# Two more buffers for raw words of w1 and w2 in the weights' pool, and the first two of their blocks converted in the fold's last four steps

## The chip, the cores and the metric

The kernel runs on one core of a Trainium2 chip. The metric is the device time of one execution in microseconds (us), the median of several runs; lower is better.

## The reference

Local attention over q, k, v (4 batches, 8 heads, 576 positions, head width 64; each position sees itself and the 63 before it), then two feed-forward layers on 2304 tokens:

```python
attn = softmax(mask(scale * q @ k.T)); x = heads side by side(attn @ v)   # 2304 x 512
x = ((x @ w1) * (x @ w2)) @ w3 @ w_out        # w1, w2: 512x1024, w3: 1024x1024, w_out: 1024x512
h = x @ w_in; out = maximum(0.01 * h, h) @ w_out2     # w_in: 512x2048, w_out2: 2048x512
```

q, k and v are float32. All weights arrive as 8-byte words (float64), so that each block of a weight is loaded twice as large as its float32 and has to be turned into float32 on the chip.

## The kernel before

Every product is made of three matmuls (`mm3`, L77, L78, L79: high x high, high x low, low x high), since each operand is split into a rounded high part and the low rest. The kernel has three stages; this case lies in the first two.

**The fold** (first 95 us). w3 @ w_out is multiplied out ahead of the tokens. It takes 16 steps (`its`); in each, `w3_tr` turns one block of w3 (TensorE L470, high part by ScalarE L472, low part by VectorE L473, both into a tile `w3T`), and `w3_mm` multiplies (tiles `mm`). The results are copied out as `wf` at L493 and L494.

**The token chunks.** Five chunks of tokens (`c` = 0 to 4), and in each eight column blocks `f`. `ab_step` multiplies x by a block of w1 (part 0, copied out by ScalarE at L669 as `a`) and of w2 (part 1, multiplied with `a` at L674, split at L675 and L676); `y_step` multiplies the result by `wf`. PSUM has two tiles `ab` for the products of `ab_step`, `w3_tr` and some transposes, taken in turn. The attention of later chunks is put between these steps by a plan (`plan_att`, `slot`): scores `sc` L245, their maximum `nm` on VectorE L249, exponent on ScalarE L253, scaling on GpSimd L263, transposes L276 copied out at L279, and the product with v L306, copied out at L309 and L310. `prep_k` (L229) and `prep_q` (L236) turn the keys and queries on VectorE after they were loaded (L224).

**Converting weights.** A block of a weight is a *unit*, numbered in order: 0 to 13 are w3 and w_out, 14 and 15 are the first 256 columns of w1 and w2, 16 and 17 the second, 18 and 19 the third, 20 and 21 the last; w_in follows. From unit 4 to 21 a unit is 1 MB of words. `advance` moves units through five steps: the load (SP's queue, L382), *scale* (ScalarE, L417 and L391, in place on the words), *shift* (VectorE, L438), *sign* (VectorE, L396), and *fin*: for w1 and w2 ScalarE writes the high part (L332) and GpSimd the low part (L333) of a tile `w`. A unit is loaded when `n_of["bits"]`, the number of units that have passed *sign*, has reached its `after` value, since it overwrites the words of an earlier one. w1 and w2 take turns in two places, `raw_at(0, 2)` and `raw_at(2, 2)`.

All loads are issued by SP, in order, on one queue. The semaphores of that queue are eight (DMAHW0 to DMAHW7), taken in turn: a load waits until the load eight places ahead of it has landed. A scheduler sets the order of the instructions on each engine when the kernel is built; each engine then runs its own list strictly in that order. The tiles' pool `wpool` has eight slots with the tag `w`: four for `wo` (w_out) and four for the first two blocks of w1 and w2; later blocks take the slots of `wo`.

Of the kernel before, what the change touches and what calls it, by code (L numbers as in the profile page):

```python
# [11 lines left out]
I64 = mybir.dt.int64  # L12
# [9 lines left out]
def tile_kernel(ctx: ExitStack, tc: tile.TileContext, q, k, v, w1, w2, w3, w_out, w_in, w_out2, out):  # L22
# [18 lines left out]
    P = 128  # L41
# [17 lines left out]
    UC = 512  # L59
# [9 lines left out]
    def f32(ap):  # L69
        return ap.bitcast(F32)  # L70
# [11 lines left out]
    wpool = tc.alloc_tile_pool(name="wpool", bufs=1)  # L82
# [229 lines left out]
    def wslot(key):  # L312
        pl, tag, bufs = wpool, "w", 8
        if key[0] == "wo2":
            pl, tag, bufs = (po1, "w1", 4) if key[1] < 4 else (po2, "w2", 4)
        elif key[0] == "wf":
            tag, bufs = "wf", 4
        return pl.tile([P, 2, 2 * UC], F32R, name=tag, tag=tag, bufs=bufs)

    def rows2(t):  # L320
        return t.rearrange("p s (l m) -> p s l m", l=2)
# [17 lines left out]
    slots = {}  # L339
# [11 lines left out]
    def part_of(kind, dims, dt=F32):  # L351

        n = 1
        for d in dims:
            n *= d
        if words_in is not None:
            return words_in.tile([P] + list(dims), dt, name=kind, tag=kind, bufs=RAW)
        i = n_of[kind] % RAW
        n_of[kind] += 1
        x = {"raw": raw_all, "f": f_all}[kind][:, i].bitcast(dt)[:, 0:n]  # L360
        return shaped(x, dims)

    def feed():

        while n_of["load"] < n_of["cap"] and n_of["bits"] >= units[n_of["load"]]["after"]:
            load_unit()
# [22 lines left out]
    def low_bits(raw, n=UC):  # L389

        act.activation(out=raw.bitcast(I32).rearrange("p (m two) -> p m two", two=2)[:, :, 0],  # L391
                       in_=raw.bitcast(U8).rearrange("p (m e) -> p m e", e=8)[:, :, 3],
                       func=AF.Copy, scale=1.0 / 32, bias=-31.0 / 64)

    def sign(f, hi):
        dve.scalar_tensor_tensor(out=f, in0=hi, scalar=-0x80000000, in1=f, op0=ALU.bitwise_and, op1=ALU.bitwise_or)  # L396

    def f_free(i):

        if i >= PHASE_B:  # L400
            return True
        a, n = units[i]["f_at"]
        for j in range(i):
            b, m = units[j]["f_at"]
            if a < b + m and b < a + n and (n_of["fin"] <= j or not units[j]["free"]()):
                return False
        return True

    def advance(stop):

        now = dict(n_of)
        if now["scale"] < min(stop, now["load"]):
            u = units[now["scale"]]
            w = u["raw"].bitcast(I32).rearrange("p (m two) -> p m two", two=2)
            u["lo"], u["hi"] = w[:, :, 0], w[:, :, 1]
            if now["scale"] < PHASE_B:
                act.mul(u["hi"].bitcast(F32), u["hi"].bitcast(F32), 2.0 ** -112)  # L417
                low_bits(u["raw"])
            else:
                u["f"] = part_of("f", [UC])  # L420
                with tc.issue_after(pss["copy"]):
                    act.mul(u["f"], u["hi"].bitcast(F32), 2.0 ** -112)
            n_of["scale"] += 1
        if now["fin"] < now["bits"]:
            u = units[now["fin"]]
            u["fin"](u["f"])
            n_of["fin"] += 1
        d = now["bits"] < now["shift"]
        if d:
            u = units[now["bits"]]  # L430
            f = u["f"].bitcast(I32)
            sign(f, u["hi"])
        if now["shift"] < now["scale"] and f_free(now["shift"]):
            u2 = units[now["shift"]]
            if now["shift"] < PHASE_B:
                i, n = u2["f_at"]
                u2["f"] = f_all[:, i:i + n].rearrange("p n m -> p (n m)")
                dve.scalar_tensor_tensor(out=u2["f"].bitcast(I32), in0=u2["hi"], scalar=3, in1=u2["lo"],  # L438
                                         op0=ALU.logical_shift_left, op1=ALU.bitwise_or)
            else:  # L440
                g = u2["f"].bitcast(I32)
                dve.tensor_scalar(g, g, 3, 0x7FFFFFF8, op0=ALU.logical_shift_left, op1=ALU.bitwise_and)
            n_of["shift"] += 1
        if d:
            if now["bits"] >= PHASE_B:
                dve.scalar_tensor_tensor(out=f, in0=u["lo"], scalar=29, in1=f, op0=ALU.logical_shift_right, op1=ALU.bitwise_or)
            n_of["bits"] += 1
            feed()
# [28 lines left out]
    def w3_mm(gi, l, half):  # L477
        t = w3T[0]
        wo = rows2(slots["wo", l // 2])
        for i in range(2 * half, 2 * half + 2):  # L480
            if l == 0:
                wps[i] = ps_mm.tile([P, DM], F32, name="mm", tag="mm")
            mm3(wps[i], t[:, 0, i, :], t[:, 1, i, :], wo[:, 0, l % 2], wo[:, 1, l % 2], l == 0, l == KF - 1)
        if half == 0:
            return
        w3T.pop(0)
        if l == KF - 1:
            for i in range(2):
                if ("wf", 2 * gi + i) not in slots:
                    slots["wf", 2 * gi + i] = wslot(("wf", 2 * gi + i))  # L490
            for i in range(4):
                wf = rows2(slots["wf", 2 * gi + i // 2])
                act.copy(wf[:, 0, i % 2], wps[i])  # L493
                dve.tensor_tensor(out=wf[:, 1, i % 2], in0=wps[i], in1=f32(wf[:, 0, i % 2]), op=ALU.subtract)  # L494
# [10 lines left out]
    def raw_at(i, n):  # L505
        return lambda: raw_all[:, i:i + n].rearrange("p n m -> p (n m)")
# [3 lines left out]
    def wf_raw(i):  # L510

        def at():
            if i not in spare_raw:
                spare_raw[i] = wpool.tile([P, 2 * UC], I64, name="wf", tag="wf", bufs=4)
            return spare_raw[i]
        return at

    for l in range(2):
        unit(w3[0:4 * P, P * l:P * l + P].rearrange("(k p) m -> p k m", p=P), (lambda l: lambda f: words.update({(0, l): f.rearrange("p (k m) -> p k m", m=P)}))(l),
             ("w3", 0, l), raw_at(2 * l, 1), 0, (2 * l, 1))  # L520
        unit(w_out[P * l:P * l + P, :], store(("wo", 0), l), ("wo", l), raw_at(2 * l + 1, 1), 0, (2 * l + 1, 1))
    PLACES = [wf_raw(0), wf_raw(1), raw_at(0, 2), raw_at(2, 2)]
    AFTER = {4: 0, 5: 0, 6: 2, 7: 4}
    for gi in range(2):
        for l in range(2 if gi == 0 else 0, KF, 2):
            i = len(units)
            unit(w3[4 * P * gi:4 * P * gi + 4 * P, P * l:P * l + 2 * P].rearrange("(k p) m -> p k m", p=P), wide_w3(gi, l),
                 ("w3", gi, l), PLACES[i % 4], AFTER.get(i, i - 3), (2 * (i % 2), 2))
            if gi == 0:
                i = len(units)  # L530
                unit(w_out[P * l:P * l + 2 * P, :].rearrange("(k p) m -> p k m", p=P), store(("wo", l // 2), None),
                     ("wo", l), PLACES[i % 4], AFTER.get(i, i - 3), (2 * (i % 2), 2))
    W12 = len(units)
    for p in range(KD):
        for w, name in ((w1, "w1"), (w2, "w2")):
            i = len(units)
            unit(w[:, 2 * P * p:2 * P * p + 2 * P].rearrange("(k p) m -> p k m", p=P), store((name, p), None), (name, p),
                 PLACES[2 + i % 2], i - 3 if i < W12 + 2 else i - 1, (2 * (i % 2), 2))
    PHASE_B = len(units)

    def keep(i):
# [6 lines left out]
                 keep(2 * p + h), ("win", p, h), None, len(units) - 1 if len(units) < PHASE_B + 2 else  # L548
                 PHASE_B if len(units) < PHASE_B + 4 else len(units) - 3)
    n_of["cap"] = KEPT = len(units)  # L550
    for name, p in [("wo", i) for i in range(4)] + [(n, p) for p in range(2) for n in ("w1", "w2")] + [("wf", i) for i in range(2)]:
        slots[name, p] = wslot((name, p))

    ev = {}
    clock = {"t": 0}
# [40 lines left out]
    def slot():  # L596

        for _, n, _, f in sorted(ev.pop(clock["t"], []), key=lambda e: e[:2]):
            with ExitStack() as how:
                if f in (av, qk, tr) and clock["t"] >= PACED_FROM:  # L600
                    how.enter_context(tc.issue_after(pss["last"]))
                if f is prep_k and n > NHP or f is prep_q and n > 2 * NHP + 1:
                    how.enter_context(tc.issue_after(pss["dve"]))
                how.enter_context(tc.high_priority(offset=100))
                f(n)
        clock["t"] += 1
# [5 lines left out]
    def start_loads(i):  # L612

        if i == W12 + 1:
            dma.append(pss["load"])
# [15 lines left out]
    its = [(gi, l) for gi in range(2) for l in range(KF)]  # L631
    until(3, W12)
    w3_tr(words.pop((0, 0)))
    w3_tr(words.pop((0, 1)))
    until(4, W12)
    for c in range(NC):
        plan_att(c)
    for i, (gi, l) in enumerate(its):
        w3_mm(gi, l, 0)
        if i + 2 < len(its):  # L640
            g2, l2 = its[i + 2]
            if l2 % 2 == 0:
                until(last["w3", g2, l2], W12)
            w3_tr(words.pop((g2, l2)))
            if l2 % 2 and g2 == 0:
                until(last["wo", l2 - 1], W12)
        slot()
        w3_mm(gi, l, 1)
        slot()
    until(W12, PHASE_B)  # L650
    p0.release()
# [579 lines left out]
```

## Time and profile before

| what | value |
|---|---|
| median of 3 runs | 815.65 us (815.35 to 817.64) |
| the profiled execution | 819.47 us, its span 817.7 us |
| TensorE (PE) busy | 785.2 us, 96% |
| VectorE (DVE) | 572.2 us, 70% |
| ScalarE (ACT) | 431.7 us, 53% |
| GpSimd (POOL) | 66.6 us, 8% |
| mean granted clock of TensorE | 0.99 |

The span is the profiled execution from its first to its last instruction; 1.8 us of its time lie around it. Its time is 3.8 us above the median, so that a sum made in the profile is carried over to the median as a difference. The granted clock is 1.0 for 2.4 GHz and 0.5 for 1.2 GHz.

### The profile page before, as it was taken

To read this page: it belongs to the slowest core of one execution; us is meant where nothing else is said; L and a number is where in the kernel's file an instruction comes from. 1 tells how busy PE (TensorE), PEld (TensorE's weight loads), DVE (VectorE), ACT (ScalarE), POOL (GpSimd) and SP (SyncE) were. 2 spreads that over 40 slices of the span, in tenths; PEclk is the share of its full clock that TensorE was granted. 3 is DMA by queue.
4 is the path that set the end of the run, shared out by engine and by line. 5 is a ranking of instruction groups with operands and counts; after the bars stand their busy time and mean duration, and the time that the engine had idled before them with its cause. 6 is when DMAs were issued, how large, how long until landed. Compare 5 with 4: busy or idle time off the path is not lost.

```text
span 817.7 us, 14546 instructions
## 1 busy us (share of the span) xinstructions
PE 785.2 (96%) x5128; PEld 724.6 (89%) x5128; DVE 572.2 (70%) x1349; ACT 431.7 (53%) x964; POOL 66.6 (8%) x61
## 2 busy tenths in 40 slices
PE   5879899999999999999999999999999999999997
PEld 4657699999988888888888899999999999999997
DVE  6995778457456546885731766867767999898976
ACT  6866675344334324443611655654556866575744
POOL 1022434112101100111000000000000000000000
PEclk9899999999999999999999999999999999999999
DMA  9995557347745556888420457998998754444321
GB/s 312 216 267 123 153 165 194 67 98 167 175 105 140 131 133 164 248 256 255 137 64 0 145 176 244 315 330 307 327 322 269 231 171 143 128 132 128 114 94 53
DMA packets 190809, 147.12 MB, mean 180 GB/s; under 512 B 124304, under 2 KB 150160, under 8 KB 190736
## 3 DMA queue, kind: packets, MB, share of 16 engines
q1 hardware_dynamic: 187712, 141.34, 59.1%
q10 hardware_dynamic: 3024, 4.85, 1.6%
q8 instruction: 40, 0.66, 0.3%
q14 instruction: 33, 0.27, 0.1%
HBM read 98.96 MB, written 47.19 MB: 179 GB/s over the span
## 4 chain that ended last, share of the span: by engine, by line
PE 78%; DMA 7%; SPq 5%; ACT 3%; DVE 2%; issue 1%; POOL 0%; ACTq 0%; DVEq 0%
PE ab L77 7%; PE o L78 7%; PE o L79 7%; PE ab L79 7%; PE ab L78 7%; PE o L77 7%; PE pr L77 6%; PE pr L79 6%; PE pr L78 6%; PE mm L78 4%; PE mm L77 4%; DMA raw<-in_moe_w_dram 4%; PE mm L79 3%; PE sc L245 3%; SPq L224 2%; SPq L623 2%
## 5 line engine op out<-in xcount | busy, mean ns | idle before, releaser
L79 PE MATMUL ab<-x,w 128*128 128x512 f32 (+1 forms) x320 | 119.9, 375 | 2.9 <-POOL w L333 2.9
L77 PE MATMUL ab<-x,w 128*128 128x512 f32 (+1 forms) x320 | 119.4, 376 | 2.0 <-ACT x L309 1.1
L78 PE MATMUL ab<-x,w 128*128 128x512 f32 (+1 forms) x320 | 119.9, 375 | 0.0
L77 PE MATMUL pr<-yop,w 128*128 128x384 f32 x300 | 101.5, 338 | 2.5 <-ACT c L826 2.5
L79 PE MATMUL pr<-yop,w 128*128 128x384 f32 x300 | 101.1, 337 | 0.0
L78 PE MATMUL pr<-yop,w 128*128 128x384 f32 x300 | 101.0, 337 | 0.0
L253 ACT ACTIVATE s<-s,nm 128x128 f32<-128x128 f32 x144 | 56.3, 393 | 47.5 <-DVE nm L249 47.5
L826 ACT COPY c<-pr 128x384 f32<-128x384 f32 x95 | 45.1, 479 | 66.2 <-PE pr L79 54.1
L78 PE MATMUL o<-yop,yop 128*128 128x256 f32 x259 | 73.1, 282 | 0.0
L79 PE MATMUL o<-yop,yop 128*128 128x256 f32 x259 | 73.0, 282 | 0.0
L77 PE MATMUL o<-yop,yop 128*128 128x256 f32 x259 | 73.0, 282 | 0.0
L79 PEld LDWEIGHTS ab<-x,w 128*128 128x128 f32 x320 | 60.5, 189 | 10.9 <-POOL w L333 3.2
L77 PEld LDWEIGHTS ab<-x,w 128*128 128x128 f32 x320 | 60.5, 189 | 10.8 <-ACT x L309 1.3
L78 PEld LDWEIGHTS ab<-x,w 128*128 128x128 f32 x320 | 60.6, 189 | 8.2 <-DVE x L310 0.3
L263 POOL TENSOR_TENSOR s<-s,rs 128x512 f32<-128x512 f32 (+1 forms) x40 | 42.4, 1062 | 291.0 <-DVE rs L262 213.1
L829 DVE TENSOR_TENSOR c<-pr,c 128x384 f32<-128x384 f32 x74 | 40.9, 554 | 31.0 <-PE pr L79 19.8
L674 DVE TENSOR_TENSOR p<-ab,a 128x512 f32<-128x512 f32 (+1 forms) x40 | 25.2, 631 | 52.3 <-PE ab L79 39.1
L968 ACT CAST yop<-raw 128x256 fp32r<-128x256 f32 (+1 forms) x92 | 42.4, 485 | 35.5 <-PE o L78 34.8
L78 PE MATMUL mm<-ab,wf 128*128 128x512 f32 (+1 forms) x160 | 59.7, 373 | 0.8 <-DVE ab L676 0.8
L77 PEld LDWEIGHTS pr<-yop,w 128*128 128x128 f32 x300 | 56.4, 188 | 3.8 <-ACT c L826 3.8
L79 PE MATMUL mm<-ab,wf 128*128 128x512 f32 (+1 forms) x160 | 59.3, 371 | 0.0
L77 PE MATMUL mm<-ab,wf 128*128 128x512 f32 (+1 forms) x160 | 56.5, 375 | 0.0
(137 smaller groups left out, 1956.9 us busy)
## 6 DMA issues: line engine op xcount, KB each, us to landing
hd<-c SPq DMA_DIRECT2D x96, 192.0 KB, 4.1
raw<-hd SPq DMA_DIRECT2D x32, 512.0 KB, 3.8
raw<-in_moe_w_dram SPq DMA_DIRECT2D x11, 1024.0 KB, 5.7
raw<-in_moe_w_out_dram SPq DMA_DIRECT2D x18, 512.0 KB, 5.3
raw<-in_moe_w_in_dram SPq DMA_DIRECT2D x16, 512.0 KB, 5.2
wd<-f SPq DMA_DIRECT2D x32, 256.0 KB, 4.1
raw<-wd SPq DMA_DIRECT2D x30, 256.0 KB, 4.4
pd<-tb SPq DMA_DIRECT2D x12, 512.0 KB, 3.0
```

What stands on the lines that cost most here:

```text
L77: pe.matmul(ps, lhsT=lh, rhs=rh, start=first, stop=False, skip_group_check=more)
L78: pe.matmul(ps, lhsT=lh, rhs=rl, start=False, stop=False, skip_group_check=more)
L79: return pe.matmul(ps, lhsT=ll, rhs=rh, start=False, stop=last, skip_group_check=more).ins
L224: sp.dma_start(dst, src)
L245: pe.matmul(sc[:, t, :], lhsT=qb[:, t, :], rhs=kT[n][:, k0:k0 + P], start=True, stop=True)
L253: act.activation(out=s[:, t, :], in_=s[:, t, :], func=AF.Exp, bias=nm[:, t:t + 1], scale=-1.0, accum_out=sm[:, t:t + 1])
L263: pool.tensor_tensor(out=s[:, 0:m], in0=s[:, 0:m], in1=rs[:, 0:m].unsqueeze(2).to_broadcast([P, m, P]), op=ALU.mult)
L623: pss["load"] = sp.dma_start(dst, src).ins
L674: dve.tensor_tensor(out=p32, in0=ps, in1=pss["a"], op=ALU.mult)
L826: pss["copy"] = act.copy(self.sb[to], ps).ins
L829: pss["add"] = dve.tensor_tensor(out=self.sb[to], in0=self.ps[at], in1=self.sb[of or to], op=ALU.add).ins
L968: tied("act", lambda: act.copy(out, x))
```

## The change

Two of the eight `w` slots of the weights' pool become buffers for raw words (`raww`). Units 16 and 17 (the second blocks of w1 and w2) are loaded into them, as soon as 12 units have passed *sign*, which is also when unit 15 may be loaded. Units 18 to 21 use the two old places again. The second blocks' tiles `w` now take slots that `wo` leaves, and the last blocks' those of the raw buffers. In each of the fold's last four steps two calls of `advance` are added, which may go as far as unit 15.

```diff
--- before.py
+++ after.py
@@ -515,6 +515,9 @@
             return spare_raw[i]
         return at
 
+    def w_raw(i):
+        return lambda: slots["raw", i]
+
     for l in range(2):
@@ -531,11 +534,13 @@
     W12 = len(units)
+    PLACES_W = [raw_at(0, 2), raw_at(2, 2), w_raw(0), w_raw(1)] + 2 * [raw_at(0, 2), raw_at(2, 2)]
+    AFTER_W = [W12 + x for x in (-3, -2, -2, -2, 1, 2, 5, 6)]
     for p in range(KD):
         for w, name in ((w1, "w1"), (w2, "w2")):
             i = len(units)
             unit(w[:, 2 * P * p:2 * P * p + 2 * P].rearrange("(k p) m -> p k m", p=P), store((name, p), None), (name, p),
-                 PLACES[2 + i % 2], i - 3 if i < W12 + 2 else i - 1, (2 * (i % 2), 2))
+                 PLACES_W[i - W12], AFTER_W[i - W12], (2 * (i % 2), 2))
     PHASE_B = len(units)
@@ -548,8 +553,11 @@
     n_of["cap"] = KEPT = len(units)
-    for name, p in [("wo", i) for i in range(4)] + [(n, p) for p in range(2) for n in ("w1", "w2")] + [("wf", i) for i in range(2)]:
-        slots[name, p] = wslot((name, p))
+    for name, p in [("wo", i) for i in range(4)] + [("raw", i) for i in range(2)] + [(n, 0) for n in ("w1", "w2")] + [("wf", i) for i in range(2)]:
+        if name == "raw":
+            slots[name, p] = wpool.tile([P, 2 * UC], I64, name="raww", tag="w", bufs=8)
+        else:
+            slots[name, p] = wslot((name, p))
@@ -646,6 +654,9 @@
         slot()
         w3_mm(gi, l, 1)
+        if i + 4 >= len(its):
+            for _ in range(2):
+                advance(W12 + 2)
         slot()
     until(W12, PHASE_B)
```

The lines below the edits have numbers up to 11 higher in the changed kernel (L669 becomes L680). The scheduler's lists move as follows.

**SP, where the loads of w1 and w2 begin.** `raw_98` are the two old places, `kin_412` the keys and `qin_413` the queries of the first visit of chunk 1. Before:

```order
L382 DMA raw_98<-in_moe_w1_dram 128x4x256 [waits DMAHW6_49,DVE_49,Activation_49]
L382 DMA raw_98<-in_moe_w2_dram 128x4x256 [waits DMAHW7_49,DVE_49,Activation_49]
L224 DMA kin_412<-in_k_dram 32x8x32 [waits DMAHW0_49]
...
L224 DMA kin_412<-in_k_dram 32x6x32 [waits DMAHW7_49]
L224 DMA qin_413<-in_q_dram 32x6x32 [waits DMAHW0_49]
```

The same place in the changed kernel:

```order
L382 DMA raw_98<-in_moe_w1_dram 128x4x256 [waits DMAHW6_49,DVE_49,Activation_49]
L382 DMA raw_98<-in_moe_w2_dram 128x4x256 [waits DMAHW7_49,DVE_49,Activation_49]
L382 DMA raww_104<-in_moe_w1_dram 128x4x256 [waits DMAHW0_49]
L382 DMA raww_105<-in_moe_w2_dram 128x4x256 [waits DMAHW1_49]
L224 DMA kin_412<-in_k_dram 32x8x32 [waits DMAHW2_49]
...
L224 DMA kin_412<-in_k_dram 32x6x32 [waits DMAHW0_49]
L224 DMA kin_412<-in_k_dram 32x6x32 [waits DMAHW1_49]
L224 DMA qin_413<-in_q_dram 32x6x32 [waits DMAHW2_49]
```

Units 16 and 17 now stand right behind 14 and 15 and ahead of the keys, and the last two of the eight loads of keys wait for them. Between the last of these eight loads and the next load of a weight stood 40 loads of queries, keys and v; now there are 38.

**SP, at that next load of a weight.** The tile `raw_98` is unit 16's words before, and unit 18's in the changed kernel; `qin_1042` and `qin_1035` are the same queries. Before:

```order
L224 DMA qin_1042<-in_q_dram 32x6x32 [waits DMAHW7_49]
L382 DMA raw_98<-in_moe_w1_dram 128x4x256 [waits DMAHW0_49,DVE_49,Activation_49]
L382 DMA raw_98<-in_moe_w2_dram 128x4x256 [waits DMAHW1_49,DVE_49,Activation_49]
L382 DMA raw_98<-in_moe_w1_dram 128x4x256 [waits DMAHW0_49,DMAHW2_49,DVE_49,Activation_49]
L382 DMA raw_98<-in_moe_w2_dram 128x4x256 [waits DMAHW1_49,DMAHW3_49,DVE_49,Activation_49]
```

In the changed kernel:

```order
L224 DMA qin_1035<-in_q_dram 32x6x32 [waits DMAHW7_49]
L382 DMA raw_98<-in_moe_w1_dram 128x4x256 [waits DMAHW0_49,DVE_49,Activation_49]
L224 DMA qin_1035<-in_q_dram 32x6x32 [waits DMAHW1_49]
L224 DMA qin_1035<-in_q_dram 32x6x32 [waits DMAHW2_49]
L382 DMA raw_98<-in_moe_w2_dram 128x4x256 [waits DMAHW3_49,DVE_49,Activation_49]
```

The rows read alike; what has moved is which unit they load.

**ScalarE, around the last turned block of w3.** `w3T_837` before and `w3T_844` in the changed kernel are the high part of the fold's last block. `w_105` before and `w_107` in the changed kernel are the first block of w2 (unit 15). L417 and L391 are the *scale* of unit 16 before and of unit 18 in the changed kernel. Before:

```order
L472 CAST w3T_837<-ab_838 128x512 [waits PE_49,Activation_49]
L417 ACTIVATE raw_98<-raw_98 128x1024 [waits DMAHW0_49]
L391 ACTIVATE raw_98<-raw_98 128x1024
L279 COPY pts_829<-ab_861 128x3x4x32 [waits PE_49]
L332 CAST w_105<-f_99 128x1024 [waits DVE_49]
L493 CAST wf_935<-mm_592 128x512 [waits PE_49]
```

In the changed kernel:

```order
L417 ACTIVATE raw_98<-raw_98 128x1024 [waits DMAHW0_49]
L391 ACTIVATE raw_98<-raw_98 128x1024
L472 CAST w3T_844<-ab_845 128x512 [waits PE_49]
L279 COPY pts_836<-ab_875 128x3x4x32 [waits PE_49]
L332 CAST w_107<-f_99 128x1024 [waits DVE_49]
L332 CAST w_1075<-f_99 128x1024
```

The last cast of a block of w3 stood ahead of the *scale* that waits for a load, and now stands behind one.

## Rows read from the trace of the kernel before

**Rows 1.** The page: busy us, share of the span and instructions of each engine

```profile
PE 785.2 (96%) x5128; PEld 724.6 (89%) x5128; DVE 572.2 (70%) x1349; ACT 431.7 (53%) x964; POOL 66.6 (8%) x61
```

**Rows 2.** Chain of waits, 48 to 110 us: start us, us, what

```profile
55.48 11.75 DMA raw<-in_moe_w_dram
67.24 0.31 SPq L224
...
88.36 0.44 SPq L224
88.91 5.55 DMA raw<-in_moe_w_dram
94.48 1.14 ACT raw L417
95.61 1.02 ACT raw L391
...
97.00 0.95 ACT w L332
...
98.02 3.42 POOL w L333
101.48 0.48 PE ab L79
```

**Rows 3.** TensorE's timeline: start, us, line, [idle before <- releaser]

```profile
23.93 2.07 PE L77 MATMUL mm<-w,w3T 128*128 128x512 f32 x4 [3.38 <-ACT w L332]
...
76.69 0.52 PE L276 MATMUL ab<-ident,s 128*128 128x128 f32 x3 [0.23 <-DVE w3T L473]
...
91.77 0.50 PE L77 MATMUL mm<-w,w3T 128*128 128x512 f32 x1
...
97.05 0.57 PE L306 MATMUL pa<-pts,x 128*64 128x64 f32 x12 [0.68 <-ACT pts L279]
97.99 0.44 PE L77 MATMUL ab<-x,w 128*128 128x384 f32 x1 [0.38 <-ACT w L332]
...
101.48 0.48 PE L79 MATMUL ab<-x,w 128*128 128x384 f32 x1 [2.87 <-POOL w L333]
...
106.17 0.44 PE L77 MATMUL ab<-x,w 128*128 128x384 f32 x1 [0.25 <-ACT a L669]
...
134.54 0.45 PE L78 MATMUL mm<-ab,wf 128*128 128x384 f32 x1 [0.76 <-DVE ab L676]
```

**Rows 4.** Engines by stretch: busy us (instructions), PEclk, DMA share, GB/s

```profile
24.00:28.00 4.00, 4.00 (x14) 3.31 (x15) 4.00 (x6) 2.74 (x3) 0.00 (x0) 0.50 1.09 324
28.00:32.00 4.00, 4.00 (x15) 3.17 (x14) 3.94 (x6) 2.74 (x4) 0.00 (x0) 0.74 1.08 269
...
62.00:64.00 2.00, 2.00 (x6) 1.59 (x5) 1.71 (x10) 2.00 (x3) 0.18 (x1) 0.50 1.04 386
...
102.00:104.00 2.00, 2.00 (x7) 2.00 (x7) 0.69 (x2) 1.29 (x2) 1.78 (x1) 0.50 0.87 338
104.00:106.00 2.00, 1.92 (x9) 1.51 (x8) 0.87 (x1) 0.74 (x2) 0.00 (x0) 0.71 0.00 0
```

**Rows 5.** SP's timeline, issues of loads: start, us, line, load, count

```profile
72.32 5.31 SPq L224 DMA_DIRECT2D qin<-in_q_dram  x11
77.73 2.84 SPq L224 DMA_DIRECT2D kin<-in_k_dram  x6
80.67 3.26 SPq L224 DMA_DIRECT2D vt<-in_v_dram  x4
```

**Rows 6.** Loads of unit 14 from issue at 54.88 to landing, in us

```profile
DMA to landing us min/median/max: 8.1/8.1/8.1
```

**Rows 7.** ScalarE's timeline around the fold's end

```profile
90.19 0.59 ACT L472 CAST w3T<-ab 128x512 fp32r<-128x512 f32 x1 [1.53 <-PE ab L470]
94.48 1.14 ACT L417 ACTIVATE raw<-raw 128x1024 f32<-128x1024 f32 x1 [3.70 <-DMA raw<-in_moe_w_dram]
...
105.63 0.48 ACT L669 COPY a<-ab 128x384 f32<-128x384 f32 x1
106.00 1.15 ACT L417 ACTIVATE raw<-raw 128x1024 f32<-128x1024 f32 x1
```

## The prediction, made before the changed kernel ran

> **What bounds the kernel now.** I read the page first: TensorE is busy for 96% of the span and the next engine, VectorE, for 70% [rows 1]. So an edit counts by the idle time of TensorE that it takes away or makes, and by what the clock does afterwards. The chain of waits names the place that the change touches [rows 2]. From 55.5 to 101.5 us it hardly runs over TensorE: it waits for a load of words (11.75 us) that lands at 67.23, follows SP issuing small loads one after another until 88.8, then one more load of words (issued at 88.91, 5.55 us), its *scale* on ScalarE (94.48 to 96.63), the cast of L332, and GpSimd's low part (98.02, 3.42 us), for which TensorE waits until 101.48. From the order of the units, the load at 88.91 is unit 16, and the low part is that of unit 15, the first block of w2.
>
> TensorE's timeline prices this place [rows 3]. It idles 0.68 us at 97.05, 0.38 at 97.99 and 2.87 at 101.48, in all 3.93 us. After that its granted clock falls to 0.50 in the stretch 102 to 104 and is 0.71 on average from 104 to 106 [rows 4]: half of the 0.52 us from 101.48 on, half of 2 us, and 0.29 of 2 us are lost, 1.8 us. So the fold's end costs 3.93 + 1.8 = 5.7 us now, and that is the prize. The other idle times up to 140 us are small: 0.23 at 76.69, 0.25 at 106.17 and 0.76 at 134.54, together 1.24 us [rows 3].
>
> The reason why unit 15 is late is to be seen on ScalarE [rows 7]. Its *scale* instruction L417 for unit 16 stood ahead of the L332 for unit 15 and waited 3.70 us for unit 16's load. That load was late because SP stood in a solid row of issues: 11 in 5.31 us, 6 in 2.84 us [rows 5], 0.48 us each.
>
> **The change part by part.** *The earlier loads.* Units 16 and 17 are now issued behind unit 15 and ahead of the keys. While three loads of words were under way, the core moved 386 GB/s [rows 4]. Two more of 1.049 MB each take 2 x 1.049 / 0.386 = 5.4 us at that rate. SP's issue of the last key load waited for unit 15 to land (67.24, right behind 67.23 [rows 2]); in the changed kernel the last key load has to wait for unit 17, at 67.24 + 5.4 = 72.7. For the upper bound I take the spacing of two landings: unit 14 was issued at 54.88 and landed 8.1 us later [rows 6], at 63.0, unit 15 at 67.23, 4.2 us apart; two of these make 8.4 us and 75.7.
>
> *What stands behind them on SP.* Everything that SP issues next is 5.4 us late: 38 loads of queries, keys and v where there were 40, then unit 18's words. I take the span that these rows had: 88.91 + 5.4 - 2 x 0.48 = 93.4 for the issue of unit 18, and 93.4 + 5.55 = 98.9 for its landing. Its own condition (unit 14 has passed *sign*) is met before that: VectorE comes to it behind the transposes of the first visit's queries, which SP issues some 30 places ahead of unit 18. The earliest end of the range: all 38 issues at 0.48 us from 72.7 + 0.4 on, with no longer one among them, 91.3, and landing at 96.9. The latest: 75.7 as the start, 96.4 and 101.9.
>
> The Trainium skill speaks for this reading (Perfetto Trace Analysis, § What "DMA-bound" means): one of the bounds that it names is the issuing engine's sequencer, seen when its track is solid with DMA slices. From 67.2 to 88.8 SP's track agrees, with an issue every 0.48 us.
>
> *What waits for unit 18.* The scheduler has put unit 18's *scale* (L417, L391) ahead of L472, the last cast of a block of w3. ScalarE runs in order, so that TensorE's last eight L77 and L78 matmuls of the fold have to wait until unit 18's words have landed and have been scaled. Before, this cast ran at 90.19, ahead of the waiting *scale* [rows 7]. Now: 98.9, plus 2.15 us for L417 and L391 (94.48 to 96.63, from the start of one to the end of both [rows 2, 7]), plus about 0.5 us for the cast: 101.6. The work that TensorE has ahead of these matmuls is the same in both kernels, and it came to them at 91.77 [rows 3]. **New idle time: 101.6 - 91.8 = 9.8 us**; at the ends 7.8 (landing at 96.9) and 12.8 (101.9). The fold itself is little disturbed before that: the keys and queries come 5.4 us later, and VectorE turns them in a stretch where TensorE still works on the fold; its low part of one block of w3 now goes ahead of these transposes, which is the 0.23 us of 76.69.
>
> *The clock behind the new stall.* It is longer than the 2.87 us idle which cost 1.8 us. After an idle time of 3.38 us (to 23.93) the clock stood at 0.50 for the whole of 24 to 28 and at 0.74 on average from 28 to 32 [rows 3, 4]: 2.0 + 1.04 = 3.0 us lost. I take 2.4, between the two, and keep 1.8 and 3.0 as ends.
>
> *What has piled up on ScalarE.* While it waits, fin of unit 15 and of unit 16 (L332, two of 0.95 us), four copies of `wf` and the *scale* of unit 19 gather; the last now stands ahead of the first copy of `a` (L680), which frees the PSUM tile of the next product. Before, that copy went first (105.63, then L417 at 106.00 [rows 7]). So the next product may be late by one more *scale*, 2.15 us, or by nothing if transposes and the rest of the first product cover it. I take 1.2, with 0 and 2.15 as ends.
>
> *What goes away.* 3.93 + 1.8 at the fold's end, since unit 15's low part will be done while TensorE does the delayed fold; and the three small ones, 1.24 (nothing of them at the upper end).
>
> **The sum.** -3.93 - 1.8 + 9.8 + 2.4 + 1.2 - 1.24 = +6.4 us. In the profile that would be 819.47 + 6.4 = 825.9; the median of the runs stands 3.8 below the profiled execution, so 815.65 + 6.4 = **822.0 us**, slower. The bounds: -5.7 + 7.8 + 1.8 + 0 - 1.24 = +2.7 (818.4), and -5.7 + 12.8 + 3.0 + 2.15 = +12.2 (827.9). After 140 us TensorE is hardly ever idle, so that nothing is won back there.
>
> **The rivals.** *Faster: the words come early enough.* If unit 18's words land by 91.77 - 2.65 = 89.1, the fold ends as before, unit 15 is ready, and the idle times go: -3.93 - 1.8 - 1.24 = -7.0, 808.7; with the ScalarE term against it, 809.9. This decides at an issue of unit 18 by 83.6, some 10 us ahead of my count. For it: two of the four loads leave the stretch behind 88.9 where they were in a row. Against it: the 38 small loads alone take SP 18 us, and they can't end before unit 17 has landed. The Trainium skill would give this case (DMA: Bandwidth & Descriptors, § Rules for kernel authors): issue a load early, compute, and wait for it late, and its fixed cost is hidden. By that rule the time is the 808.7 worked out here; the trace so far bears it out for units 16 and 17 only, since the wait moves to unit 18.
>
> *No change: the new wait is about as long as the old.* A stall of 4 us in place of 9.8, with the same clock behind it, gives 815.65 within 0.3% (2.4 us, about what a measurement of this kernel can tell from no change). It takes a landing of unit 18 near 93, an issue near 87.6, or attention work that TensorE finds while it waits. Its own list is in order as well, and the next rows on it need the same cast, which speaks against the second.
>
> *Much slower: the fold stalls too.* VectorE turns the keys ahead of another low part of `w3T`. If the two loads take far more than 8.4 us, or the small loads behind them pile up, the fold loses 3 us and more before it comes to the stall: above 828. The rate of 386 GB/s over several microseconds speaks against it.
>
> *The change does not do what it says.* Unit 15 is not finished inside the fold: its L332 stands behind unit 18's *scale*. That is part of the forecast itself; only if the low part then also came late for TensorE would it cost more, and the delayed fold covers its 3.42 us.
>
> **How the numbers follow.** Forecast (818.1 to 827.9) 0.70; faster, about 809, 0.12; no change 0.14; much slower 0.04. Slower by over 0.3% has 0.70 + 0.04 = 0.74, within 0.3% 0.14, faster 0.12. The time is the forecast's 822.0. For 8 in 10 the range takes in the forecast but its top and most of the no-change case: 814 to 827; left out are the faster case, the much slower one and a few hundredths at the top of the forecast.
>
> **What would show it.** On SP the last key load goes out near 72.7, and unit 18's words near 93.4. ScalarE idles 7 us or more ahead of an L417 that ends on a load near 99, and the cast of `w3T` follows at 101. TensorE has one idle time of 8 to 13 us there, released by L472, with a granted clock of 0.50 behind it, and none released by L333. If SP issues unit 18's words by 88, or the cast is not behind them, the forecast is wrong and the time falls to 809 to 816. If the stall is there and the total still does not rise, the mistake is in what I count as gone or in what comes later.

## The result and the profile after

The changed kernel is **slower**: median 826.13 us (822.34 to 827.04, 4 runs) against 815.86 us for the kernel before beside it, a ratio of 1.0116 with a 95% interval of 1.0093 to 1.0140, or 9.5 us. The profiled execution took 827.04 us, its span is 825.3 us, 7.6 more than the 817.7 of before.

The page says little: TensorE's busy time is that of before to 0.1 us [rows 1], so that the loss is idle time. The half clock at this place costs 0.7 us more than before, as the sum below has it; it doesn't show in the busy time because the clock of the stretches 24 to 28 and 28 to 32 us stood at 0.61 and 1.00 here, where it stood at 0.50 and 0.74 before [rows 4]. Two new idle times of 0.49 us (at 40.30 and 58.73) took most of that back: TensorE comes to the 11th block of w3 that it turns at 65.07 us, before at 65.33.

```profile
PE 785.1 (95%) x5128; PEld 723.8 (88%) x5128; DVE 574.3 (70%) x1349; ACT 431.8 (52%) x964; POOL 64.2 (8%) x61
```

TensorE's timeline, its rows with idle time from 85 to 140 us (start, us, line, in brackets the idle time before it and what ended it):

```profile
87.80 0.57 PE L306 MATMUL pa<-pts,x 128*64 128x64 f32 x12 [0.17 <-DVE x L310]
100.73 0.79 PE L77 MATMUL mm<-w,w3T 128*128 128x512 f32 x1 [9.06 <-ACT w3T L472]
112.44 0.44 PE L77 MATMUL ab<-x,w 128*128 128x384 f32 x1 [1.28 <-ACT a L680]
131.88 0.55 PE L276 MATMUL pa<-ident,s 128*128 128x128 f32 x3 [1.23 <-POOL s L263]
136.91 0.44 PE L78 MATMUL mm<-ab,wf 128*128 128x384 f32 x1 [1.53 <-DVE ab L687]
```

The three idle times at the fold's end [rows 3], 3.93 us, are gone; 9.06 us stand in their place, released by the last cast of a block of w3. The chain of waits from 87 to 104 us says why (start, us, what):

```profile
91.73 0.44 SPq L224
...
92.28 5.82 DMA raw<-in_moe_w_dram
...
98.12 1.10 ACT raw L417
99.22 0.99 ACT raw L391
100.21 0.48 ACT w3T L472
...
100.73 0.79 PE mm L77
```

Small loads on SP until 92.2, unit 18's words at 92.28, their landing at 98.10, *scale*, cast, matmul. SP's timeline has the start and the end of that row of loads; the last of the eight loads of keys ends at 72.2, where it ended at 67.55 before [rows 2]:

```profile
58.65 13.53 SPq L224 DMA_DIRECT2D kin<-in_k_dram  x8
...
92.28 0.39 SPq L382 DMA_DIRECT2D raw<-in_moe_w_dram  x1
...
93.81 24.23 SPq L382 DMA_DIRECT2D raw<-in_moe_w_dram  x2
```

ScalarE's timeline shows what stood behind the wait of 8.87 us, and that the *scale* of unit 19 (109.84, 110.86) now goes ahead of the first copy of `a`, which came first before [rows 7]:

```profile
86.41 0.59 ACT L472 CAST w3T<-ab 128x512 fp32r<-128x512 f32 x1
...
98.12 1.10 ACT L417 ACTIVATE raw<-raw 128x1024 f32<-128x1024 f32 x1 [8.87 <-DMA raw<-in_moe_w_dram]
99.13 1.08 ACT L391 ACTIVATE raw<-raw 128x1024 int32<-128x1024 uint8 x1
100.11 0.56 ACT L472 CAST w3T<-ab 128x512 fp32r<-128x512 f32 x1
100.58 0.48 ACT L279 COPY pts<-ab 128x384 f32<-128x384 f32 x1
100.95 2.00 ACT L332 CAST w<-f 128x1024 fp32r<-128x1024 f32 x2
...
109.84 1.18 ACT L417 ACTIVATE raw<-raw 128x1024 f32<-128x1024 f32 x1
110.86 1.16 ACT L391 ACTIVATE raw<-raw 128x1024 int32<-128x1024 uint8 x1
111.87 0.51 ACT L680 COPY a<-ab 128x384 f32<-128x384 f32 x1
```

The windows behind the stall (busy us and instructions of PE, PEld, DVE, ACT, POOL, then PEclk, DMA share, GB/s):

```profile
100.00:102.00 2.00, 1.27 (x3) 1.08 (x4) 0.69 (x1) 2.00 (x5) 0.00 (x0) 0.50 0.10 38
102.00:104.00 2.00, 2.00 (x6) 1.40 (x5) 0.00 (x0) 0.95 (x2) 1.92 (x1) 0.50 0.00 0
104.00:106.00 2.00, 2.00 (x17) 1.44 (x16) 0.09 (x1) 0.48 (x1) 2.00 (x2) 0.59 0.00 0
106.00:108.00 2.00, 2.00 (x12) 1.86 (x11) 0.47 (x1) 0.45 (x1) 0.80 (x1) 1.00 0.00 0
```

TensorE is busy from 100.73 to 106. It loses half of the 3.27 us up to 104, when the level is 1.2 GHz, and 0.41 of the next 2 us: 2.5 us.

The last two idle times, 1.23 and 1.53 us, stand where before had one of 0.76 [rows 3]. VectorE's timeline leads to both: one operation of 3.30 us delays L262, after which GpSimd makes the `s` that TensorE waits for at 131.88, and another of 3.31 delays L687.

```profile
126.91 3.30 DVE L396 SCALAR_TENSOR_TENSOR f<-raw,f 128x1024 int32<-128x1024 int32 x1
...
130.67 0.16 DVE L262 RECIPROCAL rs<-rs 128x3 f32<-128x3 f32 x1
...
133.07 3.31 DVE L396 SCALAR_TENSOR_TENSOR f<-raw,f 128x1024 int32<-128x1024 int32 x1
136.31 0.55 DVE L687 TENSOR_TENSOR ab<-p,ab 128x384 fp32r<-128x384 f32 x1
```

One row of before that was not shown is needed for the sum: there TensorE idled once more later, and the changed kernel has no idle time from 160 to 200 us.

```profile
168.14 0.62 PE L77 MATMUL ab<-x,w 128*128 128x384 f32 x2 [1.11 <-ACT x L309]
```

### The profile page after: what moved, and what is told of

The parts are those of the page before. It is cut to its first block, busy times and chain, and to the rows that moved or that the text cites. A ratio compares the mean times of both kernels' runs of the same rounds, so it can differ in the third digit from the quotient of the medians.

```text
span 825.3 us, 14547 instructions
## 1 busy us (share of the span) xinstructions
PE 785.1 (95%) x5128; PEld 723.8 (88%) x5128; DVE 574.3 (70%) x1349; ACT 431.8 (52%) x964; POOL 64.2 (8%) x61
## 4 chain that ended last, share of the span: by engine, by line
PE 80%; DMA 8%; ACT 4%; SPq 3%; DVE 2%; issue 2%; ACTq 0%; DVEq 0%
PE o L78 7%; PE o L79 7%; PE o L77 7%; PE ab L77 7%; PE ab L78 7%; PE ab L79 7%; PE pr L77 7%; PE pr L79 6%; PE pr L78 6%; DMA raw<-in_moe_w_dram 5%; PE mm L78 4%; PE mm L77 4%; PE mm L79 4%; SPq L224 3%; PE sc L245 3%; PE pa L306 2%
```

## The experiments

**Theory A** is that of the prediction: unit 18's *scale*, which waits for words that SP issues late, stands on ScalarE ahead of what TensorE needs next. The rivals are named in the expectations. All times are medians; each ratio is to the kernel before in the same series (815.1 to 816.2 us).

| label | edit, in short | us | ratio (95% interval) |
|---|---|---|---|
| e1_buffers_only | changed kernel, no added conversions | 823.69 | 1.0107 (1.0077 to 1.0137) |
| e2_advance_only | kernel before, added conversions | 816.79 | 1.0012 (0.9994 to 1.0029) |
| e3_cast_first | changed, last cast of w3T ahead of unit 18's *scale* | 823.75 | 1.0106 (1.0085 to 1.0126) |
| e4_fin_first | and unit 15's L332 ahead | 821.70 | 1.0087 (1.0061 to 1.0113) |
| e8_x_first | and the last visit's L309 ahead | 817.16 | 1.0013 (0.9998 to 1.0029) |
| e12_scale_after_a | changed, *scale* begun after the first copy of `a` | 814.64 | 0.9991 (0.9974 to 1.0008) |
| e5_before_fin_first | before, conversions, unit 15's L332 ahead of unit 16's *scale* | 815.21 | 0.9990 (0.9973 to 1.0008) |
| e7_pool_queries | changed, 16 query loads on GpSimd | 818.67 | 1.0024 (1.0005 to 1.0043) |
| e11_x_first_pool_queries | e8 and e7 | 817.37 | 1.0018 (1.0001 to 1.0035) |
| e13_after_a_pool_queries | e12 and e7 | 818.86 | 1.0038 (1.0019 to 1.0057) |
| e10_x_first_low_dve | e8, low parts on VectorE | 816.68 | 1.0005 (0.9988 to 1.0023) |
| e9_low_dve | changed, low parts on VectorE | 821.50 | 1.0074 (1.0048 to 1.0100) |

### Which half of the change costs: e1 and e2

```diff
 e1, against the changed kernel        e2, against the kernel before
-        if i + 4 >= len(its):         +        if i + 4 >= len(its):
-            for _ in range(2):        +            for _ in range(2):
-                advance(W12 + 2)      +                advance(W12 + 2)
```

> The changed kernel without the six added conversions in the fold's last steps; both raw buffers and the new order of loads stay. Theory A (the loss is unit 18's *scale*, which stands on ScalarE ahead of the last w3T cast and waits for words that SP issues late): that order is the same here, so TensorE still idles about 9 us ahead of the weight product at L77, and the time stays 6 to 11 us above before, 822 to 827 us. Rival B (the added conversions crowd VectorE and ScalarE in the fold's last steps, and the stall is only where this shows): without them the time falls back to before, 814 to 817 us.

> The kernel before with the added conversions alone, no new buffers: unit 16 and 17 keep their old places. ScalarE's order at the fold's end is that of before, the last w3T cast ahead of unit 16's *scale*. Theory A: the stall of before (2.87 us ahead of the 101.48 product, with what belongs to it 3.9 us) stays and nothing new comes, 814 to 817 us. Rival B (the conversions themselves cost): 820 to 827 us.

The buffers and their order of loads alone cost what the whole change does (1.0107 against 1.0116), with an idle time of 8.83 us at the same matmul; the added conversions alone change nothing that can be measured, and the stall of before stays at 2.87 us. Rival B falls.

### The order on ScalarE: e3, e4, e8, e12

The first three put more and more of ScalarE's rows ahead of unit 18's *scale*, and leave SP's line as it is:

```diff
+                with ExitStack() as how:
+                    if now["scale"] >= W12 + 4:
+                        how.enter_context(tc.issue_after(pss["cast"]))   # e3, e4, e8: L472
+                        how.enter_context(tc.issue_after(pss["fin"]))    # e4, e8: L332
+                        how.enter_context(tc.issue_after(pss["x"]))      # e8: L309
```

e12 has `issue_after(pss["copy"])` in their place, the copy of `a`, and lets no *scale* beyond unit 17 begin before it:

```diff
-    until(W12, PHASE_B)
+    until(W12, W12 + 4)
...
-                    advance(PHASE_B)
+                    advance(PHASE_B if i else W12 + 4)
```

> The changed kernel with one order changed on ScalarE: the *scale* and *bits* of units 18 and later come behind the last w3T cast, while the fin of unit 15's low part (L332) still stands behind unit 18's *scale*. Theory A: the 9.06 us ahead of the weight product go, but the weight product's later rows need the low part of unit 15, so TensorE waits there for about 4 to 8 us instead: 817 to 824 us. Rival C (the 2 MB of words for units 16 and 17 delay SP's other loads, so that keys and queries are what TensorE lacks): the stall stays near 9 us whatever ScalarE's order, 824 to 828 us.

TensorE's timeline of this kernel: the 9.06 us are gone, and the next rows on ScalarE behind unit 18's *scale* (L279 at 99.71, then L332) are what TensorE waits for.

```profile
100.23 0.85 PE L306 MATMUL pa<-pts,x 128*64 128x64 f32 x12 [4.28 <-ACT pts L279]
104.10 0.69 PE L79 MATMUL ab<-x,w 128*128 128x384 f32 x1 [1.43 <-POOL w L333]
```

The time is at the top of what theory A gave; rival C's stall near 9 us whatever the order is not there.

> As the kernel with the cast first, and unit 15's last fin (L332) ahead of unit 18's *scale* too. Theory A: nothing at the fold's end waits for unit 18 any more, so the 9.06 us stall and the half clock behind it (about 2.4 us) go; the two late stalls (1.23 and 1.53 us at 131.88 and 136.91 us) may stay. From 826.1 that gives 813 to 817 us, at best under before. Rival C (SP's loads are late for TensorE itself): over 820 us. Rival D (the buffers in the weights' slots cost elsewhere): a time over 818 us with no stall in this stretch.

The time fell, but less than theory A gave, and is over the 820 us of rival C. Its timeline shows the wait one more step down ScalarE's line, at L309, and a new kind of it behind VectorE:

```profile
98.98 0.44 PE L77 MATMUL ab<-x,w 128*128 128x384 f32 x1 [3.37 <-ACT x L309]
104.68 0.44 PE L77 MATMUL ab<-x,w 128*128 128x384 f32 x1 [1.26 <-ACT a L684]
109.62 0.69 PE L77 MATMUL ab<-x,w 128*128 128x384 f32 x1 [2.59 <-DVE p L689]
```

So it isn't SP's loads that TensorE lacks (rival C): all three are ScalarE's or VectorE's rows.

> The kernel with the fin first, and the copy of the last visit's product (L309) also ahead of unit 18's *scale*, since TensorE waited 3.37 us for it there. Theory A: no row that TensorE needs before 100 us stands behind unit 18's wait any more; the 3.37 us and part of the half clock behind it go, 3 to 6 us under the 821.7 us of the kernel with the fin first: 815.5 to 819 us. Rival F (VectorE's work on the words, slowed beside GpSimd's L333, is now what TensorE waits for in this stretch): other waits take the place, behind p at L689 and s at L249, and the time stays at 820 to 823 us.

The last step gives 4.5 us by the medians, 6.0 by the ratios, as theory A had it; rival F's 820 us and more falls. The wait for unit 18 is still there on ScalarE (1.45 us), and TensorE pays for it at the next row in that line, the first copy of `a`:

```profile
103.79 0.44 PE L77 MATMUL ab<-x,w 128*128 128x384 f32 x1 [2.98 <-ACT a L685]
```

> The changed kernel in which the *scale* and *bits* of units 18 and later are only begun after the first copy of a (L680 of the changed kernel), and so stand behind the fold's last casts, unit 15's and 16's fin, the copy of the last visit's product, the casts of wf and the first copy of a. Theory A: at that place the words have long landed, so ScalarE waits for unit 18 nowhere and TensorE's 9.06 us stall, the half clock behind it and the 1.28 us at a all go: from 826.1 down by 10 to 13 us, 813 to 816 us. If the later start of units 18 to 21 is missed after 110 us, it stays at 816 to 819 us.

814.64 us: the whole loss of the change is undone by the place of the *scale* of units 18 and later, and the time can't be told from that of before, so the buffers in the weights' slots cost nothing by themselves (rival D falls). ScalarE's timeline has the *scale* of unit 18 right behind the copy of `a`, with no wait:

```profile
97.52 0.53 ACT L683 COPY a<-ab 128x384 f32<-128x384 f32 x1
97.89 1.21 ACT L420 ACTIVATE raw<-raw 128x1024 f32<-128x1024 f32 x1
```

That first copy comes 8 us earlier than before (105.63 [rows 7]), of which 3.1 us were won ahead of this place (last table of this section); little of the rest is left at the end. TensorE's timeline shows a new idle time, which VectorE's `p` (the product with `a`) ends, and the clock falls behind it (0.55 and 0.60 in the windows 104 to 106 and 106 to 108):

```profile
102.80 0.44 PE L77 MATMUL ab<-x,w 128*128 128x384 f32 x1 [2.03 <-DVE p L688]
```

On VectorE's timeline an operation on words that took 2.87 us instead of 1.22 stands ahead of that `p` (102.20):

```profile
97.07 2.87 DVE L441 SCALAR_TENSOR_TENSOR f<-raww 128x1024 int32<-128x1024 int32 x1
```

### The same order in the kernel before: e5

> The kernel before with the added conversions, no new buffers, and on ScalarE the *scale* of units 16 and later put behind unit 15's last fin (L332). Theory A (the order on ScalarE decides what a late landing costs): TensorE's wait of 2.87 us for unit 15's low part goes; as the kernel with the fin first showed for unit 18, the wait for unit 16's words then stands ahead of the next rows in ScalarE's line, but these are needed later: 811 to 816 us. If the landing costs the same wherever its wait stands in the line, the time stays at 814.5 to 817.5 us.

The edit puts `issue_after(pss["fin"])` on the *scale* of units 16 and later in e2. Its time can't be told from that of before, 1 us under it, and lies where the ranges of the two cases overlap, so that it decides nothing. The trace says more: no idle time at the fold's end is left, and the clock is 1.00 from 94 to 116 us. What was won is given back in later waits (TensorE's timeline, the four largest):

```profile
100.05 0.45 PE L77 MATMUL ab<-x,w 128*128 128x384 f32 x1 [1.44 <-ACT a L673]
113.47 0.94 PE L245 MATMUL sc<-kT,qbd 128*128 128x128 f32 x6 [0.65 <-DVE nm L249]
119.56 0.55 PE L276 MATMUL pa<-ident,s 128*128 128x128 f32 x3 [1.14 <-POOL s L263]
...
132.10 0.44 PE L78 MATMUL mm<-ab,wf 128*128 128x384 f32 x1 [0.77 <-DVE ab L680]
```

### Unit 18's words earlier: e7, e11, e13

```diff
-        for dst, src in ls:
-            sp.dma_start(dst, src)
+        for i, (dst, src) in enumerate(ls):
+            (pool if far and i >= len(ls) // 2 else sp).dma_start(dst, src)
```

`far` holds for the loads of two visits of chunk 1, so that 16 loads of queries leave SP's line.

> The changed kernel with 16 query loads issued by GpSimd, so that unit 18's load stands 14 places earlier in SP's line, about 6 us earlier at 0.46 us each; ScalarE also gets unit 18's *scale* behind the last w3T cast. Theory A: the words land near 92 us instead of 98 and the stall of 9.06 us at the weight product goes or falls under 3 us: 815 to 820 us. Rival E (the landing isn't set by SP's line but by the traffic): the words land at 97 to 99 us anyway, and with the changed order on ScalarE the time is about that of the kernel with the cast first, 823 to 825 us.

SP's timeline, and ScalarE's, where the last cast of w3 (89.90) now precedes the wait:

```profile
88.40 6.36 SPq L382 DMA_DIRECT2D raw<-in_moe_w_dram  x2
```

```profile
89.90 0.57 ACT L472 CAST w3T<-ab 128x512 fp32r<-128x512 f32 x1
93.53 1.18 ACT L417 ACTIVATE raw<-raw 128x1024 f32<-128x1024 f32 x1 [3.06 <-DMA raw<-in_moe_w_dram]
```

The load goes out 3.9 us earlier and lands at 93.5 instead of 98.1, so SP's line does set the landing; rival E falls. That is less than the 6 us that were expected. The largest idle time from 85 to 112 us is 1.06 us, and the time falls by some 7 us; how much of that is the earlier landing and how much the changed order was not separated.

> The kernel with the copy first, and 16 query loads issued by GpSimd, which put unit 18's load at 88.4 us instead of 92.3 in the run with that edit alone. Theory A: unit 18's words land 4 us earlier, before ScalarE comes to their *scale*, and the wait of 2.98 us for the copy of a goes too: 813 to 816 us, at or under before. If VectorE's work is what bounds the stretch from 88 to 126 us by now, the time stays at 816 to 818 us.

> The kernel whose scale comes after a, and the 16 query loads on GpSimd. Theory A: with no wait for unit 18 left the earlier landing is worth nothing more, within 1 us of the kernel whose scale comes after a. If units 18 to 21 are the bound after 110 us, the earlier load gives 1 to 3 us.

Both misses of theory A. In e11 ScalarE waits for unit 18 nowhere and the clock stays at 1.00 from 94 to 116 us, and it still took 817.37 us: by now something else bounds the stretch, and the rows that end TensorE's waits there are VectorE's and GpSimd's but for one of 0.41 us. e13 is 4 us slower than e12; it has idle times of 1.46 us (for L333), 2.65 (VectorE's `x`), 1.26 (`p`) and 0.76 (`qbd`). VectorE's `x` (102.17) stands there behind an operation on words of 3.38 us (98.25). Why the same edit that helps e7 hurts e12 was not separated.

### VectorE beside GpSimd: e9 and e10

```diff
-            (pool if key[0] in ("w1", "w2") else dve).tensor_tensor(out=t[:, 1, sl], in0=f, ...
+            dve.tensor_tensor(out=t[:, 1, sl], in0=f, ...
```

> The changed kernel with the low parts of w1's and w2's blocks (L333) on VectorE instead of GpSimd, nothing else. It tests where the two late waits of the changed kernel came from (1.23 us at 131.88 and 1.53 us at 136.91, not in the prediction's sum). If they came from VectorE's operations being slowed beside GpSimd (1.22 us alone, 3.1 to 3.3 us beside it), L396 and L438 all stand at 1.22 us, the two waits go, and the time falls by 2 to 3 us to 823 to 824.5 us with the stall of about 9 us unchanged. If they came from unit 18's words and all behind them being late, the waits stay and the time stays at 825 to 828 us.

VectorE's timeline of e9, an L396 and the moved L333:

```profile
118.41 1.21 DVE L396 SCALAR_TENSOR_TENSOR f<-raw,f 128x1024 int32<-128x1024 int32 x1
...
124.68 1.22 DVE L333 TENSOR_TENSOR w<-f,w 128x1024 fp32r<-128x1024 f32 x1
```

Every L396 takes 1.21 to 1.25 us now, and L333 1.18 to 1.31 instead of 2.4 and more. TensorE's timeline keeps the stall and has no idle time between 112 and 140 us; both late waits are gone:

```profile
99.06 0.80 PE L77 MATMUL mm<-w,w3T 128*128 128x512 f32 x1 [9.31 <-ACT w3T L472]
110.14 0.44 PE L77 MATMUL ab<-x,w 128*128 128x384 f32 x1 [0.61 <-ACT a L680]
```

By the ratios (1.0116 and 1.0074) that is worth 3.4 us, where 2 to 3 were expected, and 821.50 us lies under the range given. The size is not sharp: both medians are of four runs, their intervals touch, and the scheduler also moved some rows of ScalarE.

> The kernel with the copy first, and the low part of w1's and w2's blocks (L333) made by VectorE instead of GpSimd. It adds eight operations to VectorE (about 1.2 us each if they take what its L396 takes alone, 9.8 us), and takes away the eight GpSimd rows beside which L396 and L442 took 2.8 to 3.4 us in place of 1.22. Rival F (the slowing beside GpSimd makes the late waits): L396 and L442 all stand at about 1.2 us, and the time is 2 to 4 us under that of the kernel with the copy first. If VectorE is short of time in all, the added 9.8 us make it 2 to 6 us slower.

817.16 and 816.68 us: no difference that can be measured, though the operations all stand at 1.22 us. Its timeline has one long idle time, 5.58 us at 104.34 for the first copy of `a`, which came at 103.77, 0.57 later than in e8. ScalarE's timeline shows why: the wait for unit 18 took 2.73 us, and the *scale* of unit 19, which stands behind that copy in e8 (103.57), went ahead of it here. So e10 differs from e8 in that order too, and the two medians do not price the low parts alone.

```profile
101.37 1.17 ACT L422 ACTIVATE raw<-raw 128x1024 f32<-128x1024 f32 x1
```

From there on e10 is faster. The first and the eighth copy of `a`, on ScalarE's timeline, show this for several kernels. The traces are of single executions, and these lie up to 3.6 us apart before the place of the change: TensorE comes to the 11th block of w3 that it turns at 65.33 us before and at 61.74 in e1, whose program is that of the changed kernel (65.07) up to there. So the first copy is also counted from that block:

| kernel | low parts on | 11th block, us | first, us | eighth, us | block to first | first to eighth |
|---|---|---|---|---|---|---|
| before | GpSimd | 65.33 | 105.63 | 156.17 | 40.3 | 50.5 |
| changed | GpSimd | 65.07 | 111.87 | 165.30 | 46.8 | 53.4 |
| e5 | GpSimd | 62.76 | 99.47 | 154.16 | 36.7 | 54.7 |
| e8 | GpSimd | 65.23 | 103.20 | 157.68 | 38.0 | 54.5 |
| e11 | GpSimd | 65.04 | 101.98 | 156.23 | 36.9 | 54.3 |
| e12 | GpSimd | 62.22 | 97.52 | 152.17 | 35.3 | 54.7 |
| e9 | VectorE | 61.93 | 109.58 | 159.43 | 47.7 | 49.9 |
| e10 | VectorE | 64.20 | 103.77 | 154.93 | 39.6 | 51.2 |

Where the order is mended and the low parts stay on GpSimd (e5, e8, e11, e12), the chunk begins 2 to 5 us earlier and then takes some 4 us longer. With the low parts on VectorE it takes over 3 us less than in the kernel that the edit was made to (e10 against e8, e9 against the changed kernel). That VectorE's slowed operations are what takes the gain back is read from these traces; no run shows it in the median, and e12's order with the low parts on VectorE, which would, was not tried.

## Why the prediction was right, point by point

The sum, term by term, as the two traces have it:

| term | predicted | measured | from |
|---|---|---|---|
| idle at the fold's end goes | -3.93 | -3.93 | no such row left |
| half clock behind it goes | -1.8 | -1.8 | as above |
| new idle time | +9.8 | +9.06 | row at 100.73 |
| half clock behind that | +2.4 | +2.5 | windows 100 to 106 |
| *scale* of unit 19 ahead of `a` | +1.2 | +1.28 | row at 112.44 |
| small idle times to 140 us | -1.24 | +1.69 | see below |
| after 140 us | 0 | -1.11 | row at 168.14 |
| sum | +6.4 | +7.7 | spans: 825.3 - 817.7 = 7.6 |

*The load.* Forecast: last key load near 72.7, unit 18 out at 93.4, landed at 98.9. Measured: 72.2 (its end), 92.28, 98.10. It took 5.82 us where unit 16 had taken 5.55. SP's row of issues is not quite as even as I had read it: the 40 small loads of before went out in 21.2 us (67.60 to 88.80), 0.53 us each and not 0.48, since four loads of v at 80.67 took 3.26 us [rows 5]; the 38 of the changed kernel took 0.52 each. The forecast of 93.4 used the whole span and so doesn't rest on the 0.48. e7 showed that the line on SP sets it.

*The stall.* TensorE stopped at 91.67 (100.73 - 9.06), forecast 91.77; the three steps behind the landing took 2.6 us as worked out. That the order on ScalarE turns the late landing into TensorE's time was argued from the lists; e3, e4, e8 and e12 show it. The same load, landing at 96.5 to 98.1 us in the changed kernel, e3 and e4, cost 9.06, 4.28 and 3.37 us at the row that stood next; it cost 2.98 in e8 where it landed at 98.9, and in e12 nothing, since no needed row did.

*What was mis-sized.* "What goes away" counted the three small idle times, 1.24 us, as gone. Two are (0.23 and 0.25), 0.17 came at 87.80, and the third, 0.76, grew to 1.23 + 1.53: -0.48 + 0.17 + 2.00 = +1.69. e9 shows the cause: VectorE's operations lengthened beside GpSimd's, and with the low parts off GpSimd both waits are gone. The trace of before had the sign of it (an L396 of 3.31 us at 130.45), which I had not read. Against that, the 1.11 us at 168.14 went, where I had counted on nothing, and the stall came out 0.74 shorter. So that the sum (+6.4) comes within 1.3 us of the traces (+7.7) is in part luck: 2.93 us too little and 1.85 too much mostly cancel.

*From the trace to the median.* I carried the sum over as if the profiled execution stood 3.8 us above the median in both kernels; that of the changed kernel stands 0.9 above it. So the medians lie 10.3 us apart where the traces lie 7.6 apart, and the forecast of 822.0 came out 4.1 us low by the medians and 3.1 by the ratio, with 826.13 inside the range of 814 to 827. Where those 2.7 us lie in the other executions, which ran from 822.3 to 827.0 us, stays open; the times of the 11th block in the last table show that executions differ by up to 3.6 us in the fold alone.

*The rivals.* The faster case needed unit 18 landed by 89.1; it landed at 98.10. The case of no change put the landing near 93; in e7, where it lands at 93.5 and the last cast precedes the wait, the ratio is 1.0024. The much slower case needed a fold that stalls before it comes to the wait, and TensorE got there at 91.67 as forecast. The rule of the Trainium skill that I weighed there (DMA: Bandwidth & Descriptors, § Rules for kernel authors: issue early, wait late) was borne out by its second half: e12 waits later, with the load not a place earlier, and the loss is gone. The 808.7 us worked out for that case were not reached even so: in e12's trace the new wait for `p` (2.03 us) and the half clock behind it (1.7 us by the two windows) come in the place of what went.

## What to carry to other kernels

A buffer that lets a load start early can, as here, only move the wait to the next load that has none; ask which instruction waits for that one, and what stands behind it on its in-order engine. Here the place of the *scale* of units 18 and later in ScalarE's list was worth some 10 us, and no load had to stand earlier. When a stall has been taken away, look at the rate of the stretch behind it before counting the gain: a start 2 to 5 us earlier than before was worth nothing that could be measured at the end. And when two traces are compared, see first how far apart they are before the place of the change.

## What the runs showed of the hardware

VectorE's operations on words (L396 and L438, 128x1024 int32, two inputs) take 1.22 us alone. In the changed kernel four of them began after a GpSimd L333 had, and took 2.93 to 3.31 us; in the kernel before, others that began later in an L333 took 1.34, 1.49 and 2.11. They are not slowed in proportion: all of these end 1.08 or 1.09 us after GpSimd does. GpSimd's timeline of the changed kernel:

```profile
126.57 2.56 POOL L333 TENSOR_TENSOR w<-f,w 128x1024 fp32r<-128x1024 f32 x1 [5.44 <-ACT w L332]
131.00 0.83 POOL L263 TENSOR_TENSOR s<-s,rs 128x384 f32<-128x384 f32 x1 [1.88 <-DVE rs L262]
132.62 2.69 POOL L333 TENSOR_TENSOR w<-f,w 128x1024 fp32r<-128x1024 f32 x1 [0.79 <-ACT w L332]
```

L333 ends at 129.13 and 135.31; the L396 at 126.91 and 133.07 end at 130.21 and 136.38. The Trainium skill states this (SBUF — State Buffer, § Who interferes with whom): a VectorE instruction with two inputs in SBUF contends with a GpSimd instruction that reads SBUF, and the one that comes later is blocked until the other has ended. The rows agree; I hadn't looked for it when I predicted.
